# Keys of chunks 4 to 7 turned by small transfers and VectorE instead of TensorE

## The chip, the cores and the metric

The kernel runs on one core of a Trainium2 chip. The metric is the time on the device in microseconds (us), as the median of several runs; lower is better. TensorE (PE in the rows, its weight loads PEld), VectorE (DVE), ScalarE (ACT), GpSimd (POOL) and SyncE (SP, which here only starts DMA transfers) each work through their own list of instructions in a fixed order and wait for each other through semaphores.

## What is computed

A linear-attention recurrence (4 batches, 8 heads, 768 steps, 48 features a head), whose output goes through a dense layer of width 2048 with the gate h * cos(h):

```python
for t in range(S):
    cur = np.einsum('bhd,bhe->bhde', u[None] * kt, vt)
    y[:, :, t] = np.einsum('bhd,bhde->bhe', rt, state + cur)
    state = wt[:, :, :, None] * state + np.einsum('bhd,bhe->bhde', kt, vt)
...
h = x @ w_in            # x: 3072 x 384, from y; w_in: 384 x 2048
g = h * np.cos(h)
return (g @ w_out).astype(np.float32)
```

## The kernel before

**Chunks, blocks, slots.** The 3072 rows are 24 chunks of 128 steps. Two chunks make a block (block 2 is chunks 4 and 5, block 3 is chunks 6 and 7). For the dense layer a block passes 8 slots; a slot takes 256 of the 2048 columns. Slots 0 to 15 belong to blocks 0 and 1, slots 16 to 23 to block 2, 24 to 31 to block 3, and so on.

**A slot** is, in order: `mm1` (PE, line 594: 18 matmuls into the PSUM tile `ph`), `I` (ACT, L557), `S` (DVE, L560), `N` (ACT, the sine, L573), `M` (DVE, L574), `H` (ACT, a cast, L171), `L` (POOL, L174) and `mm2` (PE, L612: 12 matmuls into `acc`), which stands two slots behind its `mm1`. Every engine has its list in this order, so `I` of a slot stands behind `H` of the slot before on ACT, and `S` behind `M` on DVE.

**A chunk's attention work**, spread between the slots' instructions: `ld`/`load` (the transfer of the tile `tt`, with the keys in its columns 512 to 1023), `e` and `f` (DVE scans, L283 and L289), `k` and `r` (DVE scales keys and queries in place, L300 and L302 from chunk 6 on), `a` (PE, scores `pa`), `A` (POOL, L335) and `P` (DVE copies by a mask, L396), `o` and `p` (PE, `py`, L479 to L513), `s` (PE, L444: keys times values, `pst`), `n` (DVE, L454: the new state `all_states`), `d` (DVE, L358), `X` (the block's output split in a high and a low part, on ACT and DVE; the low part is L174 on DVE).

**Turned keys.** `s` needs the keys with the steps on the partitions: a tile `kn`, two buffers. Two steps make it, called `t` and `K` here. Up to chunk 7 (`j < BY_BLOCKS`, L403) `t` is four TensorE transposes into a PSUM tile `pt` (L408), and `K` is a copy from there (L413, on ACT in the opening and on DVE later; the rows show it under the helper's line, L171). From chunk 8 on `t` is 16 DMA transfers of 32 by 32 blocks within SBUF, into one of two `top` tiles (L425), all started by SP, and `K` is one VectorE transpose within 32 by 32 blocks (L429). `s` is issued in the order of the chunks, so its first 32 matmuls read the first chunk's `kn` and its last 32 the second's.

**What sets the order.** `START` is a hand-written order for the opening (through slot 15); in it SP's list too is as written. From slot 16 on, `FIRST` (8 rows, for slots 16 to 23) and then `PLAN` (8 rows, repeated) give each slot's tokens; a token with `+2` or `+3` in a row of `FIRST` is for chunk 6 or 7, with `+4` or `+5` for chunk 8 or 9. There SP's list is left to a scheduler, the other engines' lists stand as written. Block 3's `o+1 p+1 s+1` stand in the row of slot 22, ahead of its `mm1`; within `p` the steps on PE are L507, then `s`, then L513.

Of the kernel before, what the change touches and what calls it, by code (L numbers as in the profile page):

```python
# [10 lines left out]
F32 = mybir.dt.float32  # L11
# [11 lines left out]
C = 128  # L23
HD = 48
NP = 4
# [40 lines left out]
START = """  # L66
ld0 e0 f0 ld1 raw2 raw1 q0 e1 k0 D14 pc0 r0 q1 cd0 v0 v1 raw0 f1 D10 a0 W0 wg2 wl2 A0 k1 pc1 wl1 r1 wy2 P0 cd1 D6 a1 wc2
t0 wg1 A1 ld3 ld2 wg0 W1 t1 P1 v5 wx2 wy1 o0 K0 K1 xh0.0 xp0.0 s0 wl0 e3 q3 wc1 xa0.0 wy0 wc0 xh0.1 wp1 f3 pc3 xp0.1
wv1 wx0 xa0.1 q2 e2 n0 k3 f2 raw3 k2 m0.0 m1.0 pc2 t3 r3 I0 r2 wg3 raw4 v2 wl3 cd2 v3 raw5 wy3 m0.1 cd3 S0 t2 a3 A3 K3
K2 A2 P3 ld7 wl4 wg4 a2 ld5 wc3 wg5 N0 raw8 raw6 P2 s1 wx3 raw9 n1 q5 o1 xh1.0 xl1.0 raw7 m1.1 xh1.1 pc5 xl1.1 M0 m0.2  # L70
wl5 Wa3 I1 wy4 m1.2 S1 m0.3 H0 cd5 wc4 N1 wy5 wc5 wg6 I2 m1.3 M1 wx4 wl6 I3 Hv1 L0 mm2.0 m0.4 wx5 S2 N2 wy6 S3 wg9 wl9
M2 m1.4 N3 L1 mm2.1 H2 I4 e5 wc6 wy9 L2 m0.5 M3 m1.5 S4 H3 wx6 N4 wg7 raw14 v4 L3 ld4 M4 raw11 m0.6 mm2.2 wl7 wcv9 wy7
wx9 mm2.3 wg8 I5 S5 wc7 wx7 H4 N5 M5 k5 m1.6 m0.7 t5 raw10 W2 wl8 wg11 I6 m1.7 H5 wy8 L4 mm2.4 S6 wc8 L5 I7 q4 N6 S7 N7
wl11 wx8 M6 mm2.5 H6 M7 H7 m0.8 m1.8 A5 wl10 L6 I8 wg10 f5 wy11 K5 m0.9 L7 S8 e4 ld6 raw13 raw12 m1.9 N8 M8 I9 wc11
wy10 wg12 wc10 mm2.6 mm2.7 raw15 d4 S9 N9 H8 r5 wx11 a5 wx10 M9 wl12 wl13 H9 L8 L9 m0.10 wy12 wc12 m1.10 wg13 m0.11 I10
k4 P5 wx12 S10 m1.11 N10 mm2.8 I11 pc4 t4 wy13 M10 wg15 wl15 Wa5 wc13 W4 d5 S11 cd4 f4 wx13 N11 K4 M11 m0.12 r4 H10 A4
L10 wg14 mm2.9 m1.12 m0.13 Hv11 wl14 I12 S12 N12 pp4 pp5 m1.13 a4 P4 wy15 L11 I13 M12 wy14 wcv15 S13 wx15 mm2.10 wc14
o2 mm2.11 N13 wx14 p2 m0.14 H12 m1.14 M13 m0.15 L12 xh2.0 Hv13 m1.15 I14 S14 N14 M14 mm2.12 I15 S15 xl2.0 L13 Hv14 L14
mm2.13 xh2.1 N15 s2 xl2.1 M15 Hv15 L15 n2
"""  # L80
FIRST = ["lr+2 lr+3 load+4 load+5 lv+4 lv+5 mm1 e+2 e+3 k+2 k+3 I S f+2 N M mm2 H L r+2",
# [7 lines left out]
LAST = "mm1 I S N M", "mm1 I S N M mm2 h l", "mm2 h l"  # L89
# [7 lines left out]
def rwkv_cos_ffn(ctx: ExitStack, tc: tile.TileContext, tr, tn, tv, u, ut, wts, w, rkw, vst, us, xs, out):  # L97
    nc = tc.nc
# [8 lines left out]
    cst = ctx.enter_context(tc.tile_pool(name="cst", bufs=1))  # L107
# [14 lines left out]
    def buf(tag, shape, dtype, name=None, pool=sb):  # L122
        return pool.tile(shape, dtype, tag=tag, name=name or tag, bufs=BUFS.get(tag, 1))
# [22 lines left out]
        nc.gpsimd.memset(past[n], 0.0)  # L146
    all_states = cst.tile([R, NG // NCB, NP, HD], F32, name="all_states")
    nc.gpsimd.memset(all_states[32:ROW], 0.0)
    quarter = cst.tile([128, 1], F32, name="quarter")
    nc.vector.memset(quarter, math.pi / 2.0)  # L150
    nc.scalar.activation(cst.tile([128, 1], F32, name="first_sine"), quarter, AF.Sin)
    tops = [buf("top%d" % n, [128, 2 * DM], I32) for n in range(2)]
# [78 lines left out]
    def part(key, run):  # L231

        assert key not in parts, key
        parts[key] = run
# [165 lines left out]
    def att_transpose(a):  # L400
        if a["c"] == NCB - 1:
            return
        if a["j"] >= BY_BLOCKS:  # L403
            turned_by_blocks(a)
            return
        pt = bank("a", [C, NP, 2, ROW], "pt")
        for p in range(NP):
            nc.tensor.transpose(out=pt[:, p].rearrange("t h d -> t (h d)")[:, :R], in_=a["k3"][:, p], identity=ident[:R, :R])  # L408

        def copied():  # L410
            a["kn"] = kn = buf("kn", [C, 4, NP, 32], F32)
            kn = kn.rearrange("t q a d -> t (q a d)")[:, :DM].rearrange("t (a h d) -> t a h d", h=2, d=HD)
            copy("kn", kn, pt[:, :, :, :HD])  # L413
            a["key"] = lambda p, h, first, m: kn[:, p, h, first:first + m]

        part(("K", a["j"]), copied)

    def turned_by_blocks(a):

        blocks = tops[a["j"] % 2].bitcast(F32)[:, :512].rearrange("p (q a t) -> p q a t", q=4, a=NP)  # L420
        keys = a["tt"][:, 512:1024].rearrange("p (a u t) -> p a u t", a=NP, u=4)
        for q in range(4):
            long = HD - 32 if q % 2 else 32
            for u in range(4):
                nc.sync.dma_start(out=blocks[32 * u:32 * u + long, q], in_=keys[32 * q:32 * q + long, :, u])  # L425

        def copied():
            a["kn"] = kn = buf("kn", [C, 4, NP, 32], F32)
            nc.vector.transpose(out=kn.rearrange("p q a d -> p (q a d)"), in_=blocks.rearrange("p q a t -> p (q a t)"))  # L429
            a["key"] = lambda p, h, first, m: kn[:, 2 * h + first // 32, p, :m]  # L430

        part(("K", a["j"]), copied)
# [205 lines left out]
    for i in PAIR:  # L638
# [7 lines left out]
                 a=att_scores, t=att_transpose, s=att_state, o=att_own, p=att_past, x=att_x)  # L646

    def att(j, n):

        whole = n in "osp"  # L650
        if not 0 <= j < (NBLK if whole else NG) or (j, n) in seen:
            return
        for m in ("decay" if n == "diag" and j < BY_PE else NEEDS.get(n, "")).split():
            for c in (range(j * BLK, (j + 1) * BLK) if whole and m not in "osp" else (j,)):
                att(c, m)
        i = j // BLK
        if n == "load":
            for m in "osp":
                att((j - BUFS["tt"]) // BLK, m)
        elif n == "t" and j < BY_BLOCKS:  # L660
            att((j - BUFS["kn"]) // BLK, "s")
        elif n == "d" and j >= NB:
            att(i - SAME, "s")
            att((j - BUFS["dd"]) // BLK, "s")
            att(i - 1, "p")
        elif n == "lv":
            att((j - BUFS["v"]) // BLK, "o")
            att((j - BUFS["v"]) // BLK, "s")
        elif n == "x":
# [128 lines left out]
    with tc.manual_schedule(engines={ET.PE, ET.DVE, ET.Activation, ET.Pool}):  # L798
# [195 lines left out]
```

## Time and profile before

| | |
|---|---|
| median of 3 runs | 499.8 us (499.64 to 502.58) |
| the profiled execution | 499.0 us, of which the span of instructions is 497.3 us |
| PE busy | 489.9 us |
| DVE / ACT / POOL busy | 388.3 / 258.1 / 204.4 us |
| granted TensorE clock | full in all of the 40 slices |

A timeline row is: start in us, length in us, engine, line, operation, result and source with shapes, count; in brackets the idle time before it and what ended it. Rows that stand for several instructions are merged, and neighbouring rows of PE overlap by the length of the pipeline, so the distance from one start to the next is the cost. The chain of waits is the work that ended last, followed back from the end: at each step to what released it.

### The profile page before, as it was taken

Reading aid. Unit: us, or ns where it says so; the run is one execution under the profiler, and the core shown is the slowest. Engines: PE = TensorE matmul, PEld = TensorE weight load, DVE = VectorE, ACT = ScalarE, POOL = GpSimd, SP = SyncE. Lnnn points to the kernel's source line nnn. Section 1 sums busy time; section 2 is a strip of 40 time slices with the busy share of each in tenths; the row PEclk is TensorE's granted clock in tenths of the full one; section 3 lists DMA queues with packets and bytes.
Section 4 is the critical chain, followed back from the end, with each engine's and each line's share of the span. In section 5 each row is a group of like instructions: output and inputs, shape, how many; then the busy total and the mean of one; then the engine's idle time right before and its main releaser. Section 6 shows DMA issues by size and latency. Waiting matters only on the chain.

```text
span 497.3 us, 13512 instructions
## 1 busy us (share of the span) xinstructions
PE 489.9 (99%) x5592; PEld 475.3 (96%) x5592; DVE 388.3 (78%) x682; ACT 258.1 (52%) x447; POOL 204.4 (41%) x274
## 2 busy tenths in 40 slices
PE   8999999999999999999999999999999999999997
PEld 7789999999999999999999999999999999999996
DVE  7999998697979869858968967966967966587633
ACT  2999888425445455445445345445535544544543
POOL 5136565235446345335343433624523633432330
PEclk9999999999999999999999999999999999999999
DMA  8993940422135153151251341333213103023001
GB/s 276 414 404 130 380 153 1 131 100 97 38 92 195 19 200 78 17 200 32 58 175 42 80 154 60 80 94 121 75 44 156 65 8 121 33 65 128 33 2 35
DMA packets 38832, 57.01 MB, mean 115 GB/s; under 512 B 23536, under 2 KB 30192, under 8 KB 38768
## 3 DMA queue, kind: packets, MB, share of 16 engines
q1 hardware_dynamic: 38624, 56.02, 33.5%
q8 instruction: 45, 0.74, 0.6%
q14 instruction: 19, 0.16, 0.1%
q10 hardware_dynamic: 144, 0.10, 0.1%
HBM read 49.02 MB, written 4.72 MB: 108 GB/s over the span
## 4 chain that ended last, share of the span: by engine, by line
PE 80%; DVE 11%; ACT 3%; DMA 2%; issue 2%; SPq 1%; POOL 1%; DVEq 0%; ACTq 0%
PE ph L594 35%; PE acc L612 34%; PE pa L382 2%; PE py L479 2%; DVE rr L560 2%; PE py L485 2%; DVE rr L574 2%; DMA raw<-wts 1%; PE py L513 1%; DVE tt L289 1%; DVE asb L396 1%; DVE ee L283 1%; PE pst L444 1%; ACT rr L557 1%; PE py L507 1%
## 5 line engine op out<-in xcount | busy, mean ns | idle before, releaser
L174 POOL TENSOR_TENSOR gs<-rr,gs 128x256 fp32r<-128x256 f32 x188 | 155.5, 848 | 225.9 <-ACT gs L171 213.2
L594 PE MATMUL ph<-xT,w 128*128 128x256 f32 x1728 | 219.6, 281 | 0.2 <-ACT xT L531 0.2
L594 PEld LDWEIGHTS ph<-xT,w 128*128 128x128 f32 x1728 | 212.3, 188 | 3.6 <-PE py L513 1.6
L612 PE MATMUL acc<-w,gs 128*128 128x384 f32 x1152 | 215.4, 337 | 0.0
L612 PEld LDWEIGHTS acc<-w,gs 128*128 128x128 f32 x1152 | 196.2, 188 | 0.5 <-issue 0.2
L573 ACT ACTIVATE rr<-rr,quarter 128x512 f32<-128x512 f32 x96 | 69.5, 724 | 90.8 <-DVE rr L560 90.8
L560 DVE SCALAR_TENSOR_TENSOR rr<-rr,ph 128x512 f32<-128x512 int32 x96 | 65.6, 684 | 54.2 <-ACT rr L557 51.2
L171 ACT CAST gs<-rr 128x512 fp32r<-128x512 f32 x91 | 56.5, 621 | 70.6 <-DVE rr L574 50.5
L574 DVE TENSOR_TENSOR rr<-rr,ph 128x512 f32<-128x512 f32 x96 | 65.0, 678 | 21.9 <-ACT rr L573 20.0
L557 ACT ACTIVATE rr<-ph 128x512 int32<-128x512 f32 x96 | 57.2, 596 | 43.5 <-PE ph L594 43.1
L335 POOL TENSOR_SCALAR_AFFINE_SELECT asb<-cd 128x512 f32<-128x512 f32 x48 | 35.3, 758 | 51.6 <-DVE cd L325 26.6
L396 DVE COPY_PREDICATED asb<-turned_mask,pa 64x128 f32<-64x128 uint8 (+1 forms) x108 | 33.6, 346 | 2.1 <-POOL asb L335 0.3
L283 DVE TENSOR_TENSOR_SCAN ee<-tt,one_e 112x516 f32<-112x516 f32 (+1 forms) x25 | 32.6, 1309 | 1.8 <-DMA tt<-tr 1.8
L289 DVE TENSOR_TENSOR_SCAN tt<-tt,inj 112x516 f32<-112x516 f32 x24 | 29.7, 1236 | 0.8
L174 DVE TENSOR_TENSOR xT<-py,xT 128x384 fp32r<-128x384 f32 x22 | 11.3, 551 | 16.6 <-ACT xT L171 16.6
L195 ACT ACTIVATE top<-raw 128x768 f16<-128x768 bf16 x16 | 17.5, 1091 | 4.2 <-DMA raw<-wts 3.6
L479 PE MATMUL py<-asb,v 128*32 128x128 f32 x384 | 18.0, 276 | 0.3 <-DVE asb L393 0.2
L485 PE MATMUL py<-asb,v 128*32 128x128 f32 x384 | 17.3, 273 | 0.0
L171 ACT CAST xT<-py 128x384 fp32r<-128x384 f32 x24 | 10.5, 481 | 12.2 <-PE py L513 8.2
L203 DVE CUSTOM_DVE_ANT_0 h<-h,top 128x1536 uint16<-128x1536 uint16 x16 | 15.7, 982 | 0.1
L171 ACT COPY past<-dd 48x192 f32<-48x192 f32 x40 | 14.0, 349 | 2.7 <-DVE dd L358 2.4
L382 PEld LDWEIGHTS pa<-tt 48*64 48x64 f32 x576 | 12.9, 133 | 2.2 <-issue 1.7
(91 smaller groups left out, 356.4 us busy)
## 6 DMA issues: line engine op xcount, KB each, us to landing
tt<-tr SPq DMA_DIRECT2D x22, 770.5 KB, 7.0
raw<-wts SPq DMA_DIRECT2D x16, 767.8 KB, 8.0
rk<-tn SPq DMA_DIRECT2D x18, 384.0 KB, 4.4
v<-tv SPq DMA_DIRECT2D x24, 224.0 KB, 3.6
ww<-w SPq DMA_DIRECT2D x6, 768.0 KB, 5.3
out<-ob SPq DMA_DIRECT2D x23, 192.0 KB, 2.1
top<-tt SPq DMA_DIRECT2D x96, 16.0 KB, 1.8
top<-tt SPq DMA_DIRECT2D x96, 8.0 KB, 1.8
```

The lines of the kernel that those rows point to most:

```text
L171: (nc.scalar.copy if E[name] is nc.scalar else E[name].tensor_copy)(out=out, in_=in_)
L174: E[name].tensor_tensor(out=out, in0=full, in1=high.bitcast(F32), op=ALU.subtract)
L283: nc.vector.tensor_tensor_scan(out=ee[:, pairs].rearrange("p a t -> p (a t)")[:, ::-1], data0=wp[:, cols][:, ::-1], data1=one_e[:, pairs]. ...
L289: nc.vector.tensor_tensor_scan(out=wp[:, 0:W129], data0=wp[:, 0:W129], data1=inj.rearrange("p a t -> p (a t)"), initial=0.0, op0=ALU.mult, ...
L335: nc.gpsimd.affine_select(out=asb, in_=col.unsqueeze(2).to_broadcast([C, NP, C]), pattern=[[0, 4], [1, C]], compare_op=ALU.is_equal, fill= ...
L396: nc.vector.copy_predicated(*(which(x) for x in (a["asb", h], turned_mask, pa[h])))
L557: nc.scalar.activation(made["rr"].bitcast(I32), ph, AF.Copy, scale=INV2PI / W_SCALE, bias=0.25)
L560: nc.vector.scalar_tensor_tensor(out=made["rr"], in0=made["rr"].bitcast(I32), scalar=-2.0 * math.pi * W_SCALE, in1=ph, op0=ALU.mult, op1=A ...
L573: N=lambda: nc.scalar.activation(made["rr"], made["rr"], AF.Sin, scale=1.0 / W_SCALE, bias=quarter),
L574: M=lambda: nc.vector.tensor_tensor(out=made["rr"], in0=made["rr"], in1=ph, op=ALU.mult), H=high, L=low)
L594: nc.tensor.matmul(out=ph[:, fi], lhsT=wgt[u * FU + fi][:, 0, a, kt * 128:(kt + 1) * 128], rhs=xT[:, b, kt], start=n == 0, stop=n == 3 * K ...
L612: nc.tensor.matmul(out=accs[i][j][:, :DM], lhsT=gs[:, a, fi, j * C:(j + 1) * C], rhs=wgt[u * FU + fi][:, 1, b], start=u == 0 and fi == 0 a ...
```

## The change

`BY_BLOCKS` goes from 8 to 4, so that chunks 4 to 7 are turned like the later ones. The `top` tiles still serve the weights when chunks 4 and 5 are turned, so these two use one new tile, `early`. `K5`, `t4`, `K4` and `t5` move in the hand-written order (`t5` to behind the last weights' transfer, ahead of `d4`), and `e6`, `k6`, `t6` go from the first row of `FIRST` into `START`; `t7` and `K7` move in `FIRST`.

```diff
-BY_BLOCKS = 8
+BY_BLOCKS = 4
...
-L10 wg14 mm2.9 m1.12 m0.13 Hv11 wl14 I12 S12 N12 pp4 pp5 m1.13 a4 P4 wy15 L11 I13 M12 wy14 wcv15 S13 wx15 mm2.10 wc14
-o2 mm2.11 N13 wx14 p2 m0.14 H12 m1.14 M13 m0.15 L12 xh2.0 Hv13 m1.15 I14 S14 N14 M14 mm2.12 I15 S15 xl2.0 L13 Hv14 L14
...
+H10 A4 L10 wg14 mm2.9 m1.12 m0.13 Hv11 K5 t4 wl14 I12 S12 N12 pp4 pp5 m1.13 a4 P4 wy15 L11 I13 M12 wy14 wcv15 S13 wx15
+mm2.10 wc14 o2 mm2.11 N13 wx14 p2 m0.14 H12 m1.14 M13 m0.15 L12 xh2.0 Hv13 e6 k6 t6 m1.15 I14 S14 K4 N14 M14 mm2.12
...
-FIRST = ["lr+2 lr+3 load+4 load+5 lv+4 lv+5 mm1 e+2 e+3 k+2 k+3 I S f+2 N M mm2 H L r+2",
+FIRST = ["lr+2 lr+3 load+4 load+5 lv+4 lv+5 mm1 e+2 e+3 k+2 k+3 I S f+2 N M mm2 H L r+2 t+3",
          "mm1 I S f+3 N M mm2 H L r+3",
-         "mm1 t+2 t+3 I S K+2 K+3 N M mm2 H L m+2 u+2 c+2 d+2",
+         "mm1 I S K+2 N M mm2 H L m+2 u+2 c+2 d+2",
...
-         "mm1 I S f+4 N M mm2 H L r+4 load+6 t+4",
+         "mm1 I S f+4 N M mm2 H L r+4 load+6 K+3 t+4",
...
+    early = cst.tile([C, 512], F32, name="early")
+    nc.gpsimd.memset(early, 0.0)
...
-        blocks = tops[a["j"] % 2].bitcast(F32)[:, :512].rearrange("p (q a t) -> p q a t", q=4, a=NP)
+        blocks = (tops[a["j"] % 2].bitcast(F32)[:, :512] if a["j"] >= ALL_OF else early).rearrange("p (q a t) -> p q a t", q=4, a=NP)
```

Lines behind the new tile's stand two further down in the changed kernel (L429 is L431 there).

On DVE, in the rows of slots 21 and 22, before: `S` of slot 21, `f8` (two rows), `M` of slot 21, `r8` (two rows), the low part of `X3`, `n3`.

```order
L560 SCALAR_TENSOR_TENSOR rr<-rr,ph 128x512
L288 RECIPROCAL inj<-ee 112x4
L289 SCALAR_TENSOR_TENSOR tt<-tt,inj 112x516
L574 TENSOR_TENSOR rr<-rr,ph 128x512
L300 TENSOR_TENSOR tt<-tt 112x256
L302 TENSOR_TENSOR tt<-tt 112x256
L174 TENSOR_TENSOR xT<-py,xT 128x384 x2
L454 TENSOR_TENSOR all_states<-pst,dd 48x192 x4
```

The same place on DVE in the changed kernel.

```order
L562 SCALAR_TENSOR_TENSOR rr<-rr,ph 128x512
L290 RECIPROCAL inj<-ee 112x4
L291 SCALAR_TENSOR_TENSOR tt<-tt,inj 112x516
L576 TENSOR_TENSOR rr<-rr,ph 128x512
L302 TENSOR_TENSOR tt<-tt 112x256
L304 TENSOR_TENSOR tt<-tt 112x256
L431 STREAM_TRANSPOSE kn<-top_102 128x512
L176 TENSOR_TENSOR xT<-py,xT 128x384 x2
L456 TENSOR_TENSOR all_states<-pst,dd 48x192 x4
```

`K7` now stands behind `M` of slot 21 and `r8`; before, it stood with `K6` three slots earlier, behind `S` of slot 18.

On DVE, at the end of the opening, before: `H` of slot 13, `S` and `M` of slot 14, `S` of slot 15, the first half of the low part of `X2`.

```order
L171 CAST gs<-rr 128x512
L560 SCALAR_TENSOR_TENSOR rr<-rr,ph 128x512
L574 TENSOR_TENSOR rr<-rr,ph 128x512
L560 SCALAR_TENSOR_TENSOR rr<-rr,ph 128x512
L174 TENSOR_TENSOR xT<-py,xT 128x384
```

The same place in the changed kernel.

```order
L173 CAST gs<-rr 128x512
L285 SCALAR_TENSOR_TENSOR ee<-tt,one_e 112x516
L302 TENSOR_TENSOR tt<-tt,ee 112x256
L304 TENSOR_TENSOR tt<-tt,ee 112x256
L562 SCALAR_TENSOR_TENSOR rr<-rr,ph 128x512
L431 STREAM_TRANSPOSE kn<-early 128x512
L576 TENSOR_TENSOR rr<-rr,ph 128x512
L562 SCALAR_TENSOR_TENSOR rr<-rr,ph 128x512
L176 TENSOR_TENSOR xT<-py,xT 128x384
```

`e6` and `k6` have come ahead of `S` of slot 14, and `K4` between `S` and `M` of that slot.

On SP, from the last weights on, before: the weights of tile 15, values, queries with keys for the diagonal (`rk`, chunks 6 and 7), `tt` of chunks 8 and 9, values, results of blocks 0 and 1, `rk` of chunks 8 and 9, then the first of the 16 blocks of chunk 8.

```order
L180 DMA raw<-wts 128x3071
L266 DMA v<-tv 128x448 x2
L262 DMA rk<-tn 128x768 x2
L248 DMA tt<-tr 128x1541 x2
L632 DMA out<-ob 128x384 x4
L425 DMA top_99<-tt 32x4x32 x4
```

The same place in the changed kernel, to the blocks of chunk 7; each chunk has four such rows of 4 transfers, of which the first of each chunk stands here.

```order
L182 DMA raw<-wts 128x3071
L427 DMA early<-tt 32x4x32 x4
L268 DMA v<-tv 128x448 x2
L264 DMA rk<-tn 128x768 x2
L250 DMA tt<-tr 128x1541
L427 DMA top_101<-tt 32x4x32 x4
L427 DMA top_102<-tt 32x4x32 x4
L634 DMA out<-ob 128x384 x2
```

There are now 16 transfers for chunk 5 between the last weights and the values, 16 for chunk 4 between these values and `rk`, 16 for chunk 6 between the two `tt`, and 16 for chunk 7, with the results of block 0 among them, ahead of the results of block 1 and the next values.

## Rows read from the trace of the kernel before

**Rows 1.** The page: span, and busy time by engine.

```profile
span 497.3 us, 13512 instructions
PE 489.9 (99%) x5592; PEld 475.3 (96%) x5592; DVE 388.3 (78%) x682; ACT 258.1 (52%) x447; POOL 204.4 (41%) x274
```

**Rows 2.** The chain of waits in order of time: start, length, what.

```profile
105.45 2.36 DVE ee L283 x2
...
174.82 2.30 PE ph L594 x18
```

**Rows 3.** Timeline of PE around the transposes of chunks 5, 4, and 6 with 7.

```profile
56.25 0.55 PE L408 MATMUL pt<-ident,tt 112*128 112x112 f32 x4
56.57 1.29 PE L594 MATMUL ph<-xT,w 128*128 128x256 f32 x9
...
78.64 0.58 PE L408 MATMUL pt<-ident,tt 112*128 112x112 f32 x4
79.23 1.30 PE L594 MATMUL ph<-xT,w 128*128 128x256 f32 x9
...
108.11 2.26 PE L594 MATMUL ph<-xT,w 128*128 128x256 f32 x18
...
112.30 2.26 PE L594 MATMUL ph<-xT,w 128*128 128x256 f32 x18
114.40 0.93 PE L408 MATMUL pt<-ident,tt 112*128 112x112 f32 x8
...
117.27 2.26 PE L594 MATMUL ph<-xT,w 128*128 128x256 f32 x18
```

**Rows 4.** Groups of instructions by line: busy us, mean ns of one, idle before.

```profile
L429 DVE STREAM_TRANSPOSE kn<-top 128x512 f32<-128x512 f32 x12 | 8.4, 699 | 0.0
```

**Rows 5.** DMA issues: what, queue, count, KB each, median us to landing.

```profile
v<-tv SPq DMA_DIRECT2D x24, 224.0 KB, 3.6
...
top<-tt SPq DMA_DIRECT2D x96, 16.0 KB, 1.8
```

**Rows 6.** Timeline of SP: values behind the last weights; ten blocks of chunk 9.

```profile
66.22 0.86 SPq L266 DMA_DIRECT2D v<-tv  x2
...
150.41 6.37 SPq L425 DMA_DIRECT2D top<-tt  x10
```

**Rows 7.** Timeline of DVE at slots 12 and 14, up to the low part of X2.

```profile
85.22 0.69 DVE L560 SCALAR_TENSOR_TENSOR rr<-rr,ph 128x512 f32<-128x512 int32 x1 [0.88 <-ACT rr L557]
...
97.85 0.69 DVE L560 SCALAR_TENSOR_TENSOR rr<-rr,ph 128x512 f32<-128x512 int32 x1 [2.86 <-ACT rr L557]
99.33 0.69 DVE L574 TENSOR_TENSOR rr<-rr,ph 128x512 f32<-128x512 f32 x1 [0.79 <-ACT rr L573]
...
101.43 0.55 DVE L174 TENSOR_TENSOR xT<-py,xT 128x384 fp32r<-128x384 f32 x1
```

**Rows 8.** Timeline of DVE: S of slots 16 and 18, copies K6 and K7, end of r8.

```profile
109.16 0.69 DVE L560 SCALAR_TENSOR_TENSOR rr<-rr,ph 128x512 f32<-128x512 int32 x1
...
117.00 0.69 DVE L560 SCALAR_TENSOR_TENSOR rr<-rr,ph 128x512 f32<-128x512 int32 x1 [0.64 <-ACT rr L557]
117.60 1.02 DVE L171 COPY kn<-pt 128x384 f32<-128x384 f32 x2
...
136.39 0.41 DVE L302 TENSOR_TENSOR tt<-tt 112x256 f32<-112x256 f32 x1
```

**Rows 9.** Timeline of ACT: I of slot 16.

```profile
106.23 0.60 ACT L557 ACTIVATE rr<-ph 128x512 int32<-128x512 f32 x1 [4.86 <-PE ph L594]
```

**Rows 10.** Timeline of PE: s of blocks 2, 3 and 4.

```profile
103.00 0.87 PE L444 MATMUL pst<-v,kn 128*32 128x48 f32 x64
103.81 0.38 PE L594 MATMUL ph<-xT,w 128*128 128x256 f32 x1
...
133.84 0.86 PE L444 MATMUL pst<-v,kn 128*32 128x48 f32 x64
...
173.06 1.16 PE L444 MATMUL pst<-v,kn 128*32 128x48 f32 x64
```

More of the change, by code (lines that the diff above doesn't have):

```diff
@@ L66 @@
 START = """
[L67 to L76, printed above, removed]
@@ L77 @@
-L10 wg14 mm2.9 m1.12 m0.13 Hv11 wl14 I12 S12 N12 pp4 pp5 m1.13 a4 P4 wy15 L11 I13 M12 wy14 wcv15 S13 wx15 mm2.10 wc14
-o2 mm2.11 N13 wx14 p2 m0.14 H12 m1.14 M13 m0.15 L12 xh2.0 Hv13 m1.15 I14 S14 N14 M14 mm2.12 I15 S15 xl2.0 L13 Hv14 L14
-mm2.13 xh2.1 N15 s2 xl2.1 M15 Hv15 L15 n2
+ld0 e0 f0 ld1 raw2 raw1 q0 e1 k0 D14 pc0 r0 q1 cd0 v0 v1 raw0 f1 D10 a0 W0 wg2 wl2 A0 k1 pc1 wl1 r1 wy2 P0 cd1 D6 a1
+wc2 t0 wg1 A1 ld3 ld2 wg0 W1 t1 P1 v5 wx2 wy1 o0 K0 K1 xh0.0 xp0.0 s0 wl0 e3 q3 wc1 xa0.0 wy0 wc0 xh0.1 wp1 f3 pc3
@@ new lines @@
+xp0.1 wv1 wx0 xa0.1 q2 e2 n0 k3 f2 raw3 k2 m0.0 m1.0 pc2 t3 r3 I0 r2 wg3 raw4 v2 wl3 cd2 v3 raw5 wy3 m0.1 cd3 S0 t2 a3
+A3 K3 K2 A2 P3 ld7 wl4 wg4 a2 ld5 wc3 wg5 N0 raw8 raw6 P2 s1 wx3 raw9 n1 q5 o1 xh1.0 xl1.0 raw7 m1.1 xh1.1 pc5 xl1.1
+M0 m0.2 wl5 Wa3 I1 wy4 m1.2 S1 m0.3 H0 cd5 wc4 N1 wy5 wc5 wg6 I2 m1.3 M1 wx4 wl6 I3 Hv1 L0 mm2.0 m0.4 wx5 S2 N2 wy6 S3
+wg9 wl9 M2 m1.4 N3 L1 mm2.1 H2 I4 e5 wc6 wy9 L2 m0.5 M3 m1.5 S4 H3 wx6 N4 wg7 raw14 v4 L3 ld4 M4 raw11 m0.6 mm2.2 wl7
+wcv9 wy7 wx9 mm2.3 wg8 I5 S5 wc7 wx7 H4 N5 M5 k5 m1.6 m0.7 raw10 W2 wl8 wg11 I6 m1.7 H5 wy8 L4 mm2.4 S6 wc8 L5 I7 q4
@@ new lines @@
+N6 S7 N7 wl11 wx8 M6 mm2.5 H6 M7 H7 m0.8 m1.8 A5 wl10 L6 I8 wg10 f5 wy11 m0.9 L7 S8 e4 ld6 raw13 raw12 m1.9 N8 M8 I9
+wc11 wy10 wg12 wc10 mm2.6 mm2.7 raw15 t5 d4 S9 N9 H8 r5 wx11 a5 wx10 M9 wl12 wl13 H9 L8 L9 m0.10 wy12 wc12 m1.10 wg13
+m0.11 I10 k4 P5 wx12 S10 m1.11 N10 mm2.8 I11 pc4 wy13 M10 wg15 wl15 Wa5 wc13 W4 d5 S11 cd4 f4 wx13 N11 M11 m0.12 r4
+H10 A4 L10 wg14 mm2.9 m1.12 m0.13 Hv11 K5 t4 wl14 I12 S12 N12 pp4 pp5 m1.13 a4 P4 wy15 L11 I13 M12 wy14 wcv15 S13 wx15
+mm2.10 wc14 o2 mm2.11 N13 wx14 p2 m0.14 H12 m1.14 M13 m0.15 L12 xh2.0 Hv13 e6 k6 t6 m1.15 I14 S14 K4 N14 M14 mm2.12
@@ L80 @@
+I15 S15 xl2.0 L13 Hv14 L14 mm2.13 xh2.1 N15 s2 xl2.1 M15 Hv15 L15 n2
 """
-FIRST = ["lr+2 lr+3 load+4 load+5 lv+4 lv+5 mm1 e+2 e+3 k+2 k+3 I S f+2 N M mm2 H L r+2",
+FIRST = ["lr+2 lr+3 load+4 load+5 lv+4 lv+5 mm1 e+2 e+3 k+2 k+3 I S f+2 N M mm2 H L r+2 t+3",
          "mm1 I S f+3 N M mm2 H L r+3",
[1 row of a table removed]
[1 row of a table added]
          "mm1 I S m+3 u+3 N M mm2 H L c+3 d+3 lr+4",
          "a+2 a+3 mm1 P+2 P+3 I S e+4 N M mm2 H L k+4",
[1 row of a table removed]
[1 row of a table added]
          "o+1 p+1 s+1 mm1 load+7 lv+6 lv+7 X+1 n+1 I S N M mm2 H L m+4 u+4 c+4 d+4",
```

## The prediction

> **What bounds the kernel now.** I read the page first: PE is busy 489.9 of 497.3 us [rows 1], so a matmul taken out is worth its own length, and anything that makes PE wait costs its full length. The chain of waits says where PE has no room to give: from 105 to 174 us it leaves PE and runs through DVE, ACT and POOL, and comes back to it at 174.82 [rows 2]. PE is busy there too; but DVE's work in that stretch ends only just in time, and this is where chunks 6 and 7 are turned. So the timeline of PE gives the price of what goes, and the timelines of DVE and SP decide whether the new path is in time.
>
> **What goes.** A transpose's cost is the distance from start to start. Chunk 5's four hold PE from 56.25 to 56.57, 0.32 us; chunk 4's from 78.64 to 79.23, 0.59 us. For the eight of chunks 6 and 7 the pair of `mm1` and `mm2` in which they stand takes 112.30 to 117.27, 4.97 us, against 4.19 us for the pair before it (108.11 to 112.30), 0.78 us [rows 3]. Together 1.69 us of PE. ACT loses two copies, which were not on the chain; DVE loses the copies K6 and K7, 1.02 us [rows 8].
>
> **What comes: 64 transfers on SP.** The ten blocks of chunk 9 took 6.37 us to issue, 0.64 us each [rows 6], and a block lands 1.8 us after its issue [rows 5]. So one chunk costs SP 10.2 us, and its keys are there 12 us after its start. Chunk 5: SP has finished the last weights at 66.2 [rows 6], so its blocks are there at 78.2. K5 stands behind a cast on DVE, in the 0.88 us in which DVE waits for ACT ahead of 85.22 [rows 7]; it takes 0.70 us [rows 4] and fits there. Cost nothing; without that gap it would be 0.70 us on DVE.
>
> Chunk 4 shares the tile with chunk 5, so its first transfer waits for K5, until 85.2 at the latest; its last block lands at 97.2. PE, 0.91 us early by then, lets `S` of slot 14 start at 97.85 - 0.91 = 96.94; `e6` and `k6` ahead of it take about 1.9 us (worked out below) of the 2.86 us that DVE waited there [rows 7]. K4 can start 0.60 us after that `S`, at 97.5, and ends at 98.2; `M` of the slot cannot start before 99.33 - 0.91 = 98.4, since it waits for the sine [rows 7]. So K4 is hidden as well, by 0.3 us in its landing. Values and `rk` behind these transfers come some 10 us later than before, but the values are used just ahead of block 3's `s` at 133.84 [rows 10], and `rk` behind slot 18, whose `S` stands at 117.00 [rows 8]. The blocks of chunk 6 are issued by about 108, those of chunk 7 (with four results between) by about 120, and their K stand at 114 and later. Nothing there is late by its transfer.
>
> **What moves, and where it bites.** `e6` and `k6` leave the queue of DVE at 105 us. There two scans took 2.36 us [rows 2] and the four scalings behind them the rest up to 109.16 [rows 8], 1.35 us; half of both goes, 1.86 us. Everything there follows `s2` on PE, which is 0.91 us early. So `S` of slot 16 starts at 109.16 - 0.91 - 1.86 = 106.4; `I` ahead of it is no hindrance, done at 106.23 + 0.60 - 0.91 = 105.9 [rows 9]. That is 2.8 us earlier. In slot 18 PE's own `mm1` limits: it ends at 114.40 - 0.91 = 113.5 [rows 3], with `I` (0.60) and about 0.2 us of passing on `S` is at 114.3 instead of 117.00, 2.7 us earlier [rows 8]. From there to slot 21 each step waits for one that has itself moved (`d6` on DVE, the copies and `I` on ACT, `A7` on POOL, `P7` on DVE), so I carry the 2.7 us on.
>
> K7 now stands behind `r8`, the last row of which ended at 136.80 [rows 8]. With 2.7 us off it starts at 134.1 and ends at 134.8. The matmuls that read it are the second half of `s` of block 3. PE reached that `s` at 133.84 [rows 10]; with 1.69 us off it is there at 132.15, and at 132.58 after its first half (0.86 / 2). **PE then waits for K7 from 132.6 to 134.8, 2.2 us**, and behind it in PE's list stand the rest of `p3` and `mm1` of slot 22, so the whole kernel waits. Before, K7 was done at 118.6 [rows 8].
>
> The bounds of this wait: DVE may keep less than 2.7 us of its lead. If it moves only as much as PE (1.69 us), K7 ends at 135.8 and the wait is 3.2 us; with the 0.91 us that block 2's `s` gives, 4.0 us. It could be 1.2 us if the lead grew by another us. Nothing is in sight that would end it wholly, since K7 would have to be 2.2 us earlier still.
>
> **Given back.** After the wait DVE stands closer to PE than before. In block 4 the `s` took 1.16 us instead of 0.86 [rows 10], since its second half came just as its `kn` was being made; DVE then is 1 us or more better placed, so these 0.3 us go.
>
> **The sum.** 497.3 - 1.69 + 2.2 - 0.3 = 497.5 us of span. The profiled execution has 499.0 us around its 497.3, so 499.2; the median of the runs is 499.8, 0.8 above the profiled one, and on that scale I forecast 500.0 us: no change that a measurement of this kernel can tell, which takes about 1%, 5 us.
>
> **Rivals.** First, the gain stays: K7 is in time after all, because DVE's work between 118 and 134 us closes up by more than what precedes it. For it: much of that work is waits of DVE for ACT, which might shrink. Against it: ACT waits in turn for DVE in every slot. The time is 499.8 - 1.7 - 0.3 = 497.8. Chance 0.17.
>
> Second, DVE gives its lead back before slot 21 and only moves with PE: a wait of 3.2 to 4.0 us, 499.8 - 1.7 + 3.2 to 4.0 = 501.3 to 502.1. For it: the shift rests on each step being released by one that has moved, and one unmoved transfer or `ph` between would hold it. Chance 0.21.
>
> Third, slower beyond doubt: the blocks of chunk 4 land late. K4 stands ahead of `M` of slot 14 and of the low part of `X2`, without which `mm1` of slot 16 cannot start. From that `M` to the end of the low part DVE takes 101.98 - 99.33 = 2.65 us [rows 7]; PE comes to that `mm1` at 103.81 - 0.91 = 102.9 [rows 10]. So K4 must start by 102.9 - 2.65 - 0.70 = 99.55, 2.3 us after the landing worked out above; from there every us costs one. If each issue took twice as long (1.27 us), the last block would land at 107.3, 7.8 us too late: 499.8 + 7.8 - 0.9 = 506.7, less what DVE's lead then saves at K7, up to 2. Against it are the ten issues that took 0.64 us each. Chance 0.04.
>
> [...] Chance 0.01.
>
> **How the numbers follow.** My forecast has the remaining 0.57, with 499.0 to 501.0 as its own range. Eight in ten lie from 497.6 (the gain kept whole) to 502.0 (the longer wait at K7). All cases but the last two lie within 5 us of 499.8: within 1% 0.94, slower 0.04 (the third and fourth, and a little of it could still stay within), faster 0.02, for a gain in the opening that I don't see.
>
> **What would show it.** In the changed profile: no L408 for chunks 4 to 7; `mm1` of slot 16 about 0.9 us earlier; `S` of slots 16 to 21 2.7 us earlier; at the second half of block 3's `s` an idle PE of about 2.2 us, released by DVE's transpose into `kn`, and the chain of waits going through it; `mm1` of slot 22 about 0.5 us later than before, and everything behind it too. K5 and K4 without a wait of DVE for a transfer. I am wrong if PE does not wait there, or if it waits ahead of 105 us for K4 or for the low part of `X2`.

## The result and the profile after

| | before | changed |
|---|---|---|
| median time, us | 500.06 (13 runs beside the changed kernel) | 503.71 (13 runs, 501.90 to 504.71) |
| ratio, 95% interval | 1 | 1.0065, 1.005 to 1.008 |
| profiled execution: time, span, us | 499.0, 497.3 | 504.16, 502.4 |

The changed kernel is 3.3 us slower by the ratio (0.65%; the two medians differ by 3.65 us): within the 1% forecast as the likeliest, but 1.7 us above the top of the range of 497.6 to 502.0. The page of the changed kernel, against [rows 1] (line numbers are two higher than before), and its row on the DMA queue that it calls `instruction` (packets, MB, share of the DMA engines), needed further down:

```profile
PE 490.8 (98%) x5576; PEld 476.1 (95%) x5576; DVE 390.7 (78%) x684; ACT 257.7 (51%) x445; POOL 207.4 (41%) x275
...
q8 instruction: 45, 0.74, 0.6%
```

PE has 16 matmuls fewer and is busy 0.9 us longer: something made matmuls that were there before take longer. The timeline of PE at block 3's `s`, against the second row of `s` in [rows 10] (start, length, what, and in brackets the idle time before it and its releaser):

```profile
133.83 0.53 PE L446 MATMUL pst<-v,kn 128*32 128x48 f32 x32
136.52 0.53 PE L446 MATMUL pst<-v,kn 128*32 128x48 f32 x32 [2.17 <-DVE kn L431]
136.99 1.11 PE L515 MATMUL py<-tt,past 48*32 48x128 f32 x32
138.02 3.43 PE L596 MATMUL ph<-xT,w 128*128 128x256 f32 x18
141.29 2.26 PE L614 MATMUL acc<-w,gs 128*128 128x384 f32 x12
```

The wait for K7 is there, 2.17 us long. What follows it is new: from the start of L515 to the start of L614 it is 141.29 - 136.99 = 4.30 us; the same work took 137.44 - 134.63 = 2.81 us before. The windows of 2 us of the same stretch show why (busy us and records of PE, PEld, DVE, ACT and POOL, then PEclk, the granted clock of TensorE, then DMA share and GB/s):

```profile
134.00:136.00 2.00, 0.35 (x34) 0.21 (x20) 2.00 (x5) 0.62 (x1) 0.59 (x2) 1.00 0.18 24
136.00:138.00 2.00, 1.48 (x64) 1.05 (x64) 0.47 (x1) 0.00 (x0) 1.40 (x2) 0.74 0.14 21
138.00:140.00 2.00, 2.00 (x17) 1.98 (x10) 1.34 (x4) 0.86 (x2) 0.00 (x0) 0.50 0.10 13
140.00:142.00 2.00, 2.00 (x16) 2.00 (x16) 1.01 (x3) 0.51 (x1) 0.00 (x0) 0.91 0.17 23
142.00:144.00 2.00, 2.00 (x15) 2.00 (x15) 1.09 (x2) 0.81 (x2) 0.00 (x0) 1.00 0.10 13
```

Behind the idle stretch of 2.17 us the granted clock of TensorE is 0.50 for 3.4 us by these windows (0.74, 0.50 and 0.91 of 2 us each), and the work behind the wait takes 4.30 - 2.81 = 1.49 us more. Of the 13 runs 11 show a mean granted clock of 0.996 or 0.997 (median 503.88 us); the two at 1.000 took 501.90 and 502.89 us.

The third loss is in rows that wait for nothing the profile shows (`issue` in the brackets; such rows are called stops below). PE in blocks 4, 5 and 9 of the changed kernel:

```profile
176.70 0.87 PE L446 MATMUL pst<-v,kn 128*32 128x48 f32 x64
177.50 0.42 PE L515 MATMUL py<-tt,past 48*32 48x128 f32 x7
178.21 0.64 PE L515 MATMUL py<-tt,past 48*32 48x128 f32 x25 [0.30 <-issue]
...
217.79 0.51 PE L596 MATMUL ph<-xT,w 128*128 128x256 f32 x2
218.48 2.03 PE L596 MATMUL ph<-xT,w 128*128 128x256 f32 x16 [0.19 <-issue]
...
373.54 0.44 PE L515 MATMUL py<-tt,past 48*32 48x128 f32 x14
374.43 0.59 PE L515 MATMUL py<-tt,past 48*32 48x128 f32 x18 [0.45 <-issue]
```

The kernel before has one clear stop of this kind, in block 5:

```profile
213.16 0.51 PE L513 MATMUL py<-tt,past 48*32 48x128 f32 x17
214.15 0.45 PE L513 MATMUL py<-tt,past 48*32 48x128 f32 x15 [0.48 <-issue]
```

What it costs is read from start to start of the `mm2` groups (L612 before, L614 after) on both sides of a place:

| `mm2` group | before | changed | difference | what lies between |
|---|---|---|---|---|
| first of all | 40.55 | 42.03 | +1.48 | the opening of this execution |
| ahead of block 3 | 129.45 | 129.44 | -0.01 | transposes gone: -0.39, -0.32 and -0.70, small steps -0.08 |
| behind block 3 | 137.44 | 141.29 | +3.85 | wait for K7 +2.37 from start to start, half clock +1.49: +3.86 |
| ahead of block 4 | 168.68 | 172.31 | +3.63 | one `mm2` of before (at 154.19) took 0.22 longer: -0.22 |
| behind block 4 | 176.96 | 180.99 | +4.03 | new stop +0.70, wait for K9 gone -0.30 |
| behind block 5 | 216.76 | 220.35 | +3.59 | the stop of before -0.8, a shorter one +0.36: -0.44 |
| ahead of block 9 | 364.76 | 368.36 | +3.60 | nothing |
| behind block 9 | 372.75 | 377.17 | +4.42 | new stop +0.82 |
| last | 485.35 | 489.77 | +4.42 | nothing |

The opening is not the change's: ACT waits longer for the first weights there (3.6 us in one wait of before, 4.7 us in three of the changed kernel), and runs below whose program is the same up to this point have their first `mm2` anywhere from 40.78 to 42.97. Without it the difference is 4.42 - 1.48 = 2.94 us at the last `mm2`, close to the 3.3 us of the ratio.

### The profile page after: what moved, and what is told of

It is laid out like the page before. It is cut to its first block, busy times and chain, and to the rows that moved or that the text cites. A ratio compares the mean times of both kernels' runs of the same rounds, so it can differ in the third digit from the quotient of the medians.

```text
span 502.4 us, 13563 instructions
## 1 busy us (share of the span) xinstructions
PE 490.8 (98%) x5576; PEld 476.1 (95%) x5576; DVE 390.7 (78%) x684; ACT 257.7 (51%) x445; POOL 207.4 (41%) x275
## 4 chain that ended last, share of the span: by engine, by line
PE 87%; DVE 5%; DMA 3%; ACT 2%; SPq 1%; issue 1%; POOL 0%; DVEq 0%; ACTq 0%
PE ph L596 39%; PE acc L614 37%; DMA tt<-tr 2%; PE pa L384 2%; PE py L481 2%; PE py L487 2%; PE py L515 1%; PE pst L446 1%; DVE rr L562 1%; PE py L509 1%; DVE ee L285 1%; PE pa L376 1%; SPq L250 1%; DVE rr L576 1%; PE pc L313 1%
## 5 line engine op out<-in xcount | busy, mean ns | idle before, releaser
L176 POOL TENSOR_TENSOR gs<-rr,gs 128x256 fp32r<-128x256 f32 x188 | 158.1, 861 | 227.9 <-ACT gs L173 216.1
L596 PE MATMUL ph<-xT,w 128*128 128x256 f32 x1728 | 220.6, 282 | 0.4 <-issue 0.2
L596 PEld LDWEIGHTS ph<-xT,w 128*128 128x128 f32 x1728 | 213.4, 189 | 4.0 <-PE py L515 2.0
L614 PE MATMUL acc<-w,gs 128*128 128x384 f32 x1152 | 215.1, 337 | 0.0
L614 PEld LDWEIGHTS acc<-w,gs 128*128 128x128 f32 x1152 | 196.2, 188 | 0.3 <-issue 0.2
L337 POOL TENSOR_SCALAR_AFFINE_SELECT asb<-cd 128x512 f32<-128x512 f32 x48 | 36.4, 782 | 52.7 <-DVE cd L327 28.5
```

Of the source, the lines that this page charges most:

```text
L176: E[name].tensor_tensor(out=out, in0=full, in1=high.bitcast(F32), op=ALU.subtract)
L337: nc.gpsimd.affine_select(out=asb, in_=col.unsqueeze(2).to_broadcast([C, NP, C]), pattern=[[0, 4], [1, C]], compare_op=ALU.is_equal, fill= ...
L596: nc.tensor.matmul(out=ph[:, fi], lhsT=wgt[u * FU + fi][:, 0, a, kt * 128:(kt + 1) * 128], rhs=xT[:, b, kt], start=n == 0, stop=n == 3 * K ...
L614: nc.tensor.matmul(out=accs[i][j][:, :DM], lhsT=gs[:, a, fi, j * C:(j + 1) * C], rhs=wgt[u * FU + fi][:, 1, b], start=u == 0 and fi == 0 a ...
```

## The experiments

**K7 right behind S.** The row of the order for slot 21, with K7 moved from behind `r8` to behind `S`:

```diff
-         "mm1 I S f+4 N M mm2 H L r+4 load+6 K+3 t+4",
+         "mm1 I S K+3 f+4 N M mm2 H L r+4 load+6 t+4",
```

> The changed kernel with one token moved: K7 stands right behind S of slot 21, ahead of f8, so about 3.2 us earlier in VectorE's list (132.53 + 0.60 against 135.77). Theory one (the loss is the wait for K7 and the lower clock behind it): K7 ends at 133.8, the second half of block 3's s begins at 134.3 without a wait, the granted clock stays full between 130 and 150 us, and 2.2 + 1.5 = 3.7 us go: about 3.7 us under the changed kernel, ratio to before 0.998 to 1.001. Theory two (the loss lies in the opening: the new tile, or transfers that crowd SP's queue): the wait goes, and the time too by its 2.2 us, but 1.5 to 2 us over before remain: ratio 1.003 to 1.005.

499.36 us, ratio 0.9994 (0.9978 to 1.0011), against 1.0065 with K7 where the change put it. Timeline of PE, then of DVE:

```profile
132.84 0.86 PE L446 MATMUL pst<-v,kn 128*32 128x48 f32 x64
133.64 0.67 PE L515 MATMUL py<-tt,past 48*32 48x128 f32 x32
134.24 2.37 PE L596 MATMUL ph<-xT,w 128*128 128x256 f32 x18
136.44 2.25 PE L614 MATMUL acc<-w,gs 128*128 128x384 f32 x12
```

```profile
132.15 0.70 DVE L431 STREAM_TRANSPOSE kn<-top 128x512 f32<-128x512 f32 x1
```

`s` runs through, and L515 to L614 takes 2.80 us again. So both the wait and the half clock come from one token's place on DVE, and no transfer held K7 up there: counted from block 2's `s` (102.79 here, 103.78 in the changed kernel) it started 29.4 us behind it instead of 32.0. Yet the kernel is not measurably faster than before. From `mm2` to `mm2`, block 4 took 8.71 us instead of the 8.28 of before, since PE now waited 0.41 us for K9; block 9 took 8.76 instead of 7.99, with a stop of 0.37 us; block 5 took 8.38 instead of 8.79, its stop being shorter and behind the run.

**K7 ahead of r8**, a smaller step: behind `M`, ahead of `mm2`.

```diff
-         "mm1 I S f+4 N M mm2 H L r+4 load+6 K+3 t+4",
+         "mm1 I S f+4 N M K+3 mm2 H L r+4 load+6 t+4",
```

> K7 one step earlier than in the changed kernel: behind M of slot 21, ahead of r8, 0.67 us. If the wait sets the time, the idle stretch of TensorE ahead of the second half of s is 2.17 - 0.67 = 1.5 us, and the time falls by at least 0.67 us. Whether the granted clock behind it still falls is open: if it does, only 0.67 us are gained, if it does not, 0.67 + 1.5 = 2.2 us.

501.64 us, ratio 1.0025 (1.0012 to 1.0039). PE:

```profile
137.01 0.54 PE L446 MATMUL pst<-v,kn 128*32 128x48 f32 x32 [1.50 <-DVE kn L431]
137.47 0.67 PE L515 MATMUL py<-tt,past 48*32 48x128 f32 x32
138.07 2.37 PE L596 MATMUL ph<-xT,w 128*128 128x256 f32 x18
140.28 2.25 PE L614 MATMUL acc<-w,gs 128*128 128x384 f32 x12
```

The wait is 0.67 us shorter and the work behind it is back at 2.81 us, with PEclk 1.00 in every window of 2 us from 134 to 144. Together 2.16 us; measured 2.1. A wait shortened by a third took the half clock away with it.

**The tile alone**: the kernel before with the tile `early` and its memset, nothing else.

> The kernel before with nothing but the new tile and its memset on GpSimd, which no one reads. Theory two: the places of the other tiles in SBUF or the 0.5 us on GpSimd make the opening slower by 1 to 2 us: ratio 1.002 to 1.004. Theory one: no difference, ratio 0.999 to 1.001; the 1.7 us that the profiled opening of the changed kernel lost by 35 us are then a matter of the one execution.

499.61 us, ratio 0.9992 (0.9982 to 1.0003): the tile costs nothing.

**The wait filled with small matmuls**: chunk 6's half of block 3's `s` issued six times over, so that PE has work while K7 is made.

```diff
-        for n, a in enumerate(two):
+        for n, a in (*(((0, two[0]),) * 5 if i == 3 else ()), *enumerate(two)):
```

> The changed kernel, with the first half of block 3's s (chunk 6, 32 matmuls, 0.43 us) issued six times over instead of once; the result is the same numbers. TensorE then works through most of the 2.17 us in which it waited for K7. Theory one: nothing is gained on the wait itself, but the granted clock stays full and L515 and mm1 of slot 22 behind it take 0.6 and 2.2 us instead of 1.03 and 3.27: 1.5 us under the changed kernel. Rival: the clock falls for another reason than the idle stretch (low activity of the small matmuls, or something that runs at that time), and the time is that of the changed kernel.

501.90 us, ratio 1.0049 (1.0028 to 1.007). The median is near the 502.2 us of theory one, but the profiled execution took 505.14 us, one of three above 504 among ten runs, and in it PE stood still all the same. PE, and windows:

```profile
133.84 2.32 PE L446 MATMUL pst<-v,kn 128*32 128x48 f32 x172
138.57 1.27 PE L446 MATMUL pst<-v,kn 128*16 128x48 f32 x52 [2.42 <-issue]
```

```profile
138.00:140.00 2.00, 1.43 (x62) 1.28 (x70) 0.00 (x0) 0.00 (x0) 0.00 (x0) 0.66 0.13 16
140.00:142.00 2.00, 2.00 (x37) 1.61 (x22) 0.57 (x2) 0.86 (x2) 0.00 (x0) 0.50 0.21 33
```

This trace does not tell the theories apart. The seven other runs, 501.19 to 502.20 us at a mean granted clock of 0.999 or 1.000, speak for theory one, but none of their traces is at hand. The trace gave two leads: the clock fell to 0.50 behind an idle PE that waited for no K7, and a run of small matmuls stopped for 2.42 us with nothing shown that it waited for.

**The wait filled with large matmuls**, seven of 128x128 by 128x128 into the part of `pst` that chunk 7's `s` overwrites; PE's stream gets 14 records more.

```diff
         for n, a in enumerate(two):
+            if i == 3 and n == 1:
+                for again in range(7):
+                    nc.tensor.matmul(out=pst[:, 1].rearrange("t a d -> t (a d)")[:, :C], lhsT=ident, rhs=ident, start=True, stop=True)
```

> The changed kernel, and between chunk 6's and chunk 7's half of block 3's s seven fp32 matmuls of 128x128 by 128x128 that write into the accumulator of chunk 7 and are overwritten by its s (two records of about 0.15 us each, 9.1 us in 60 records: 7 x 0.30 = 2.1 us), so that PE works through the 2.17 us in which it waited for K7; nothing of the computation is left out. Theory one (the wait itself stays, and what comes on top of it comes from a PE that stood idle): K7 starts as late as before, so the second half of s stays at about +2.2 us behind the first, but the granted clock stays at 1.00 in every 2 us between 134 and 146, the L515 group and the ph behind it take the 2.81 us that they took in the kernel before and not 4.30, and the time is 1.5 us under the changed kernel's 503.7: about 502.2, ratio to the kernel before 1.0035 to 1.0055. Theory two (the fall of the clock comes with the place or with the small matmuls and not with the idle time): clock about 0.5 at 138 to 140 again, 503.7 or more. Theory three (no part of the loss lies here): 503.7 with the clock full. A count beside it: the fourteen added records move every later matmul by 14 places in PE's stream, so the stop that waits for nothing shown, after 7 of the 32 matmuls of L515 in block 4 and after 14 of 32 in block 9, should leave these two places if it hangs on the place in the stream, and come in block 5 after about 20 of 32.

500.51 us, ratio 1.0012 (1.0002 to 1.0022). PE, and one window:

```profile
132.74 0.53 PE L449 MATMUL pst<-v,kn 128*32 128x48 f32 x32
133.20 1.83 PE L443 MATMUL pst<-ident 128*128 128x128 f32 x14
135.43 0.54 PE L449 MATMUL pst<-v,kn 128*32 128x48 f32 x32 [0.41 <-DVE kn L431]
135.90 0.67 PE L518 MATMUL py<-tt,past 48*32 48x128 f32 x32
136.50 2.40 PE L599 MATMUL ph<-xT,w 128*128 128x256 f32 x18
138.73 2.25 PE L617 MATMUL acc<-w,gs 128*128 128x384 f32 x12
```

```profile
138.00:140.00 2.00, 2.00 (x16) 2.00 (x15) 1.90 (x6) 0.60 (x1) 0.00 (x0) 1.00 0.20 28
```

K7 is as late as before: the halves of `s` start 2.69 us apart here and in the changed kernel. But PE was at work, the clock stayed at 1.00, and the work behind took 2.83 us instead of 4.30. None of the ten runs shows a mean granted clock under 0.998. With K7 behind `S`, where the same small matmuls ran without the idle time at a clock of 1.00, this shows that the idle time brings the half clock here. The time fell by more than the 1.5 us expected: the 14 records also moved the stops, as the expectation's count foresaw. The passages of blocks 4 and 9 (from the start of the `mm2` ahead of a block to that of the `mm2` behind it) fell from 8.68 and 8.81 us to 7.99 and 7.99. The stop foreseen in block 5 came too: the passage took 8.46 us, and PEld stopped after 21 of the 32 weight loads:

```profile
214.63 0.17 PEld L518 LDWEIGHTS py<-tt,past 48*32 48x32 f32 x11 [0.34 <-issue]
```

**The count moved, nothing else**: the kernel with K7 behind `S`, and four or fifteen tiny matmuls (8 or 30 records) in the opening. A place in PE's stream at which a stop falls if it hangs on the count is called a block boundary here.

```diff
             for again in range(j):
                 nc.tensor.matmul(out=filled, lhsT=ident, rhs=ident, start=True, stop=True)
+            if j == 6:
+                for again in range(4):        # or 15
+                    nc.tensor.matmul(out=filled[:32, :1], lhsT=ident[:, :32], rhs=ident[:, :1], start=True, stop=True)
```

> The kernel with K7 behind block 3's S, and four more small fp32 matmuls (32 weights' columns, 1 moved column, written over by nothing that is read) in the opening, eight records, about 0.1 us. It shows whether PE's stop in block 9, which waits for nothing that the profile shows (0.37 us after 14 of the 32 matmuls of L515, 0.77 us against the kernel without it), hangs on the count of instructions ahead of it. [...] Theory two (it hangs on the place in the program or on another engine): after 14 of 32 in block 9 as before, none in block 5. Time within 0.3 us of 499.4 on one look either way.

> As the run with four, but with fifteen small matmuls, thirty records, about 0.4 us in an opening in which PE waits 0.36 us and more behind them. Theory one (stops hang on the count): every block boundary of PE's stream moves 30 matmuls earlier against the program; in block 4 it falls 57 matmuls into the 112 of L509, L446 and L515, in block 5 84 in, in block 6 111 in, in blocks 7 to 9 10, 37 and 64 in, so the stop of 0.77 us in block 9 is gone, and at most a smaller one comes in block 5 after 4 of 32 matmuls of L515: time 0.3 to 0.8 us under the kernel with K7 behind S (499.4), 498.6 to 499.2, ratio 0.9975 to 0.999. Theory two (not the count): the stop in block 9 stays, 499.4 to 499.8.

With four, PE in block 5 and in block 9:

```profile
215.92 0.41 PE L515 MATMUL py<-tt,past 48*32 48x128 f32 x6 [0.24 <-issue]
...
371.73 0.42 PE L515 MATMUL py<-tt,past 48*32 48x128 f32 x6
372.46 0.65 PE L515 MATMUL py<-tt,past 48*32 48x128 f32 x26 [0.31 <-issue]
```

With fifteen, in the opening and in block 6 (none in blocks 5 and 9):

```profile
36.62 0.30 PE L487 MATMUL py<-asb,v 128*32 128x128 f32 x2 [2.48 <-issue]
...
255.52 0.66 PE L515 MATMUL py<-tt,past 48*32 48x128 f32 x31
256.70 0.29 PE L515 MATMUL py<-tt,past 48*32 48x128 f32 x1 [0.52 <-issue]
```

Block 5 stops after 26 of 32 and block 9 after 6, each 8 places earlier than with K7 behind `S` alone (block 9 after 14 of 32, block 5 two matmuls behind its 32); with fifteen, block 6 stops after 31, which is place 111 of the 112 matmuls of L509 (16), L446 (64) and L515 (32), as expected. The places follow the count. The forecast of the time failed: 503.93 us with fifteen (1.0091, 1.007 to 1.0111), and 501.95 with four in its one run. I had counted the places in blocks 4 to 9 alone; in the opening, where the small matmuls come in an even longer run, a stop now fell inside them. PE stood 2.48 us there (1.15 us with four) and its granted clock behind it was 0.50, and its first `mm2` started at 45.20 us (43.70 with four) instead of 40.78. From the first `mm2` to the last the kernel with fifteen took 443.56 us against 444.15 with K7 behind `S` alone, 0.59 less: over that stretch the forecast of 0.3 to 0.8 us held.

**The count put back in the changed kernel**: eight of the 16 matmuls of the first half of block 2's `s` issued twice, 16 records, as many as the transposes had. Beside it the changed kernel once more.

```diff
+                        for again in range(2 if i == 2 and n == 0 and p < 2 else 1):
                             nc.tensor.matmul(out=pst[to:to + m, n, p], lhsT=a["key"](p, h, first, m),
                                              rhs=a["v"][:, at:at + HD], start=True, stop=True)
```

> The changed kernel, with eight of the sixteen matmuls of the first half of block 2's s issued twice (they write the same values again; sixteen records, 64 such records take 0.87 us, so about 0.2 us). These stand for the sixteen transposes' records that the change took out of PE's stream, so that every later instruction is again about as far along in the stream as before the change; nothing else is undone. Theory one (the stops that wait for nothing shown hang on the count, and the change made them worse by 1.08 us: 0.70 us new in block 4 and 0.82 in block 9, 0.44 gone in block 5): the stop of block 4 after 7 of 32 and that of block 9 after 14 of 32 are gone, one in block 5 comes back after 17 or 18 of 32, as in the kernel before, and the time is 0.9 us under the changed kernel run beside it; the wait for K7 and the half clock behind it stay, 2.2 and 1.5 us. Theory two (the stops have another cause, such as DVE's or SP's changed order): places and time as in the changed kernel, plus 0.2 us.

> The changed kernel itself, for a comparison on the same chip and in the same rounds as the run with the count restored. Its rows have stops after 7 of 32 matmuls of L515 in block 4 and after 14 of 32 in block 9, a wait of 2.17 us for K7 and half clock behind it, and it took 503.7 us, 1.0065 of the kernel before: the same is expected by every theory, with 502 to 505 us for single runs, since the length of the opening varies by about 1.5 us between executions.

502.08 us (1.0037, 1.0023 to 1.0051) against 503.71 us (1.0068, 1.0054 to 1.0081) beside it: 1.6 us less, where 0.9 was expected. Blocks 4 and 9 pass in 7.99 us each; the changed kernel beside it took 9.25 and 8.82, its stop in block 4 being 0.83 us this time, not 0.30. Block 5 has its stop again (8.52 us; PEld stops after 19 of the 32 weight loads). The wait for K7 (2.16 us) and the half clock stayed in its trace, as they should.

**Both mends**: K7 behind `S`, and the count put back.

> The two mends together: K7 right behind S of slot 21's block, so that PE waits for it no more, and eight of the sixteen matmuls of the first half of block 2's s issued twice (they write the same values again), so that PE's stream counts as before the change. From rows: against the kernel before, 0.47 us less PE time up to slot 16 and 0.79 in slot 18, 0.2 us more for the repeated matmuls, block 4's wait for K9 about 0.1 longer, and one stop in block 5 of about 0.5 us where before had 0.8, none in block 9: about 1.2 us under the kernel before, 498.7, ratio 0.9965 to 0.9985. If the count of instructions has no part in the time, it stands where the kernel with K7 behind S stood, 0.9994 plus 0.2 us: 0.9998.

498.82 us, ratio 0.9981 (0.9971 to 0.999): faster than both kernels, by little. PE in blocks 3, 5 and 9:

```profile
133.42 0.87 PE L447 MATMUL pst<-v,kn 128*32 128x48 f32 x64
134.21 0.67 PE L516 MATMUL py<-tt,past 48*32 48x128 f32 x32
...
212.35 0.62 PE L516 MATMUL py<-tt,past 48*32 48x128 f32 x18
213.52 0.45 PE L516 MATMUL py<-tt,past 48*32 48x128 f32 x14 [0.55 <-issue]
...
369.33 0.67 PE L516 MATMUL py<-tt,past 48*32 48x128 f32 x32
```

No wait in block 3, one stop after 18 of 32 in block 5 (17 in the kernel before), none in block 9. This is the gain that the change could have had: about 1.0 us.

## Why the prediction missed

**What goes: right.** 0.39 + 0.32 + 0.70 = 1.41 us were saved where the transposes stood, 1.69 forecast. Where DVE is just as late as PE, a little comes back as a wait: with K7 behind `S`, PE waits 0.20 us for DVE at the place where chunk 4's transposes stood.

**What comes: right in effect, mis-sized in one term.** An issue on SP took 0.71 to 0.78 us here, not 0.64, but nothing was late by it. DVE turned K5 and K4 without waiting for a transfer, 0.70 us each. No run shows a slow turning, which has a chance of 0.01 in the forecast: the blocks of 16 KB for `early` and `top` landed in 1.8 us. SP, then DVE:

```profile
67.31 11.33 SPq L427 DMA_DIRECT2D early<-tt  x16
...
99.03 12.45 SPq L427 DMA_DIRECT2D top<-tt  x16
```

```profile
85.04 0.70 DVE L431 STREAM_TRANSPOSE kn<-early 128x512 f32<-128x512 f32 x1
...
99.23 0.70 DVE L431 STREAM_TRANSPOSE kn<-early 128x512 f32<-128x512 f32 x1
```

**What moves: right.** Counted from block 2's `s` (103.00 before, 103.78 after), `S` of slot 16 came 1.67 us earlier (108.27 against 109.16), 1.86 forecast, and K7 started 31.99 us behind it (135.77); the forecast was 134.1 against an `s` at 103.00 - 0.91, which is 32.0. The wait was 2.17 us against 2.2. DVE:

```profile
108.27 0.69 DVE L562 SCALAR_TENSOR_TENSOR rr<-rr,ph 128x512 f32<-128x512 int32 x1
...
135.77 0.70 DVE L431 STREAM_TRANSPOSE kn<-top 128x512 f32<-128x512 f32 x1
```

**The sum: here it failed.** Its premise was that "anything that makes PE wait costs its full length". So it put down the wait at its own length, "2.2", and went on as if PE came out of it as it went in. A term was missing: the granted clock of 0.50 that came behind the idle PE, 1.49 us. The rows of the kernel before could not price it, since PE never stood that long in the middle of the kernel, but the page has the granted clock, and a forecast that makes the bounding engine idle should have kept a margin for it. The same holds for the second rival, whose longer waits were priced by length alone too.

**A second term that I did not see at all**: the stops, 0.70 + 0.82 - 0.44 = 1.08 us. The 16 transposes were counted as time on PE only; they are also instructions in PE's stream.

Put together: 0.2 (the sum as forecast) + 1.49 + 1.08 + 0.28 (saving 1.41 instead of 1.69) = 3.05 us, against 2.94 at the last `mm2` and 3.3 by the ratio. What is left is 0.17 us by which the wait was longer from start to start (2.37), and small steps of -0.08 and -0.22. The wait for K9 went as forecast (block 4's `s` took 0.87 us instead of 1.16).

The rival that the gain stays did not come true as the change was written, and even with K7 in time the kernel stood at 0.9994, not 2.0 us lower: the longer wait for K9 (0.43 us) and the stop of block 9 (0.77 us, against 0.41 us less in block 5) took part of the gain.

The forecast also took about 1% as the least change that can be told on this kernel. The interval of 1.005 to 1.008 tells 0.65% from none.

## What to carry to other kernels

Price a wait that you put on the bounding engine by its length and by what follows it: here 2.17 us of waiting brought 1.49 us more. Look at the granted clock behind the idle stretches (here it fell behind some of 1.15 to 2.48 us), and fill such a stretch, or shorten it, before anything else. Where a token may stand at several places of an order, put it as soon as its input is there and its reader's deadline allows, not at the end of the row. In this unrolled stream, 16 matmuls fewer and 8, 14, 16 or 30 records more each moved the stops in the long runs of small matmuls; compare the "issue" rows of both kernels before a difference is put down to the change itself.

## What the runs showed of the hardware

**Half clock behind an idle PE.** Idle 2.17 us (changed kernel), 2.42 us and 2.48 us (the two "issue" stops): the granted clock behind it was 0.50 for 3.4 us by the windows of 2 us. Idle 1.50 us at K7, or 0.41 us with large matmuls ahead: it stayed at 1.00. But with four tiny matmuls in the opening it fell behind a stop of 1.15 us too, in a stretch where PE had also waited 0.21 us for DVE. Nor did every run of the changed kernel show it: two of 13 had a mean granted clock of 1.000. So the length of one wait does not decide alone; what does was not settled.

**Stops by the count.** PE's records come in pairs, a weight load and a matmul (x5576 each on the page), and blocks 3 to 8 have 480 pairs each from one L509 to the next. The matmuls of L509, L446 and L515 stand in a run of 16 + 64 + 32 = 112. In the changed kernel the stops stand at place 87 in block 4 (16 + 64 + 7), 114 in block 5 (two matmuls of L596 behind the run) and 94 in block 9. From block 4 to block 5 the place moves on by 27, from block 4 to block 9 by 7. Five blocks at 27 would be 135, which is 7 + 128: an estimate from these three stops is that the places come round every 128 pairs, 256 records (or a whole part of that). By the 480 pairs of a block alone they would move on by 4 x 128 - 480 = 32, not 27, so the estimate needs 5 pairs a block that the records don't show. With these two numbers every other place comes out: the boundary of block 3 falls at place 87 - 27 = 60, the next one 128 further, at 188, and the run of small matmuls that filled the wait stopped after 16 + 172 = 188. The 160 extra pairs of that run put the boundary of block 6 at place 87 - 160 + 128 + 2 x 27 = 109, and there its L515 stopped after 29 of 32 (0.4 us), which is 109.

Boundaries at places 86 to 114 of such a run mostly cost 0.36 to 1.3 us (0.08 us in block 5 of the changed kernel run again), at one after 188 PE was idle 2.42 us, and a boundary at place 84 (block 5 with fifteen tiny matmuls) or below cost nothing that shows. Nor was there a stop at place 87 of block 4 with K7 behind `S`, where PE had waited 0.41 us for K9 a little ahead of it.

The row of the queue `instruction` has 45 packets in 0.74 MB, 16 KB each, one about every 11 us (45 in 502 us). The four stops of the kernel before and of the changed kernel that are shown above, at 214.15, and at 178.21, 218.48 and 374.43 us, ended 1.31, 1.21, 1.50 and 1.29 us after a packet of this queue had landed. Ahead of the last of them one packet started at 372.20 us and landed at 373.14. The row of the queue from 372.1 to 373.2 us:

```profile
q8 instruction: 1, 0.02, 5.3%
```

The trace does not say which engine a packet was for, nor what PE waits for in a stop: the cause of the stops was not shown. That they hang on the count is shown.
